# Zeros written into alpha's layout, an early ScalarE table load, and wider filler matmuls in a fused linear-attention, DFT-mixing and feed-forward kernel

## The chip, the core and the metric

The kernel runs on one core of a Trainium2 chip. Its engines are TensorE (PE in the profile; PEld is its weight load), VectorE (DVE), ScalarE (ACT), GpSimd (POOL) and SyncE (SP, which here only issues DMAs). Each takes its instructions in order from its own queue and waits on semaphores for the others. The metric is the device time of one execution in microseconds, lower being better.

## The reference, cut to what matters

```python
# attention: q, k, v, alpha are (4, 8, 768, 48); alpha lies in 0.8 .. 1.0
for t in range(768):
    state = alpha[:, :, t, :, None] * state + einsum('bhd,bhe->bhde', k[:, :, t], v[:, :, t])
    y[:, :, t] = einsum('bhd,bhde->bhe', q[:, :, t], state)
# x = y as (4, 768, 384)
mixed = real(fft(fft(x, axis=1), axis=2))
u = x + mixed
un = (u - mean(u)) / sqrt(var(u) + 1e-06)          # over the last axis
out = u + maximum(un @ w_ch1, 0.0) @ w_ch2         # 384 -> 1536 -> 384
```

## The kernel before, in words

**Tiling.** Two heads of one batch make a pair: head one on partitions 0 to 47, head two on 64 to 111 (`CW = 112` in all), time along the free axis (768 steps). There are 16 pairs, four to a batch. The recurrence is worked in chunks of `C = 64` steps. `products` (L666) builds the running product of alpha within each chunk by a scan on DVE (`w<-al,d` in the profile), then a second scan runs backwards through the alpha tile and overwrites it in place (`al<-al,back`). For both, alpha at the first step of each chunk has to be zero, so that a chunk starts afresh, and its true values have to stand in `d1`. The kernel before makes this on the chip: it copies the 12 first-step values (stride 64) into `d1`, on ACT (on DVE for pair 0), and then sets them to zero in the tile with a memset, on POOL (on DVE for pair 0). Pair 0 is loaded and worked in two halves of 384 steps.

**The check.** The scans divide by products, so the kernel first looks whether alpha is in a safe range: an ACT Square with an accumulator reads the top byte of each alpha (`c<-al,cm` in the profile, with a short instruction that reads the accumulator) and sums (top byte - 63) squared into a column of `bad`. If the sum of all is not zero, a slow general path runs after the fast one. For pairs 1 to 15 the check stands ahead of `products`; for pair 0, `check_first` (L572) loads alpha a second time into an `h` tile and checks that.

**Stages.** `attn_stages` gives a pair's stages: the scans, the products with k and q on DVE, PE transposes of k evacuated by ACT (`kt<-a`), the matmuls inside a chunk (`f<-w,al`, masked by POOL's affine_select on the copied `x`), chunk states (`f<-vn,kt`, then `tt` on DVE) and the output `y`. `mix_stages` stores the time-reversed half of y to DRAM (`scr<-y`) and gathers it back with three indirect DMAs on POOL (`y<-scr,rows`), and does both DFTs. `norm_stages` normalizes, and `ffn_stages` runs the two feed-forward matmuls (`f<-x,wt`, then `f<-wt,h`) with weights that `wsplit` prepares on ACT, DVE and POOL.

**What sets the order.** Nothing is issued as written. `Plan` (L174) records every operation with a key and an estimated duration, and `emit` (L358) lays them out on a clock of its own, engine by engine, taking what can start first and among those the lowest key. DMA bytes are costed by `wire` (L347), 400 KB per us for rows of 512 bytes and more. So a changed estimate can change the order on any engine. All instructions are issued from one helper line, L471.

**Fillers.** In the first `WARM = 120` planned us, where the plan has a gap on PE, `emit` (L430 to L432) puts `int(gap / DUMMY)` filler matmuls of zeros ahead of the next PE operation, counted at `DUMMY = 0.11` us each (the lambda at L1130, so they have their own line in the profile). A filler is an fp32 matmul and shows as two records. They write to a part of a PSUM tile that holds no result.

**The start.** On the SP queue stand, in this order: the two halves of alpha and k of pair 0, its q, its v (`vn`), then alpha, k and q, v of pairs 1, 2, 3. The ACT queue issues two small DMAs of constants. DVE begins with `setup` (L604): memsets, the first of which is `zero`, the fillers' operand.

Of the kernel before, what the change touches and what calls it, by code (L numbers as in the profile page):

```python
# [10 lines left out]
F32 = mybir.dt.float32  # L11
# [3 lines left out]
U8 = mybir.dt.uint8  # L15
I8 = mybir.dt.int8
AF = mybir.ActivationFunctionType
# [3 lines left out]
B, H, S, D = 4, 8, 768, 48  # L21
DM = H * D
DFF = 4 * DM
P = 128
NT = S // P
NP2 = H // 2
C = 64
# [3 lines left out]
CW = 112  # L31
GRP = 64
VW = NT * H // NP2 * D + GRP - D
EVAC = 5000.0
NY = 5
NAL = 4
NQK = 2
NVN = 2
# [10 lines left out]
KM = 410.0  # L49
FB = 1  # L50
PARTS = (6, 6)
SPLIT = 388
KCK = -700.0
KF0 = -505.0
WARM = 120.0
MARGIN = 0.8
DUMMY = 0.11
KTINY = 0.5 * 2.0**15 / (1.0 + 15.5 / 128.0)


# [113 lines left out]
class Plan:  # L174
# [20 lines left out]
    def fixed(self, tile):  # L195
        return View(Slot(None, tile))
# [150 lines left out]
    def wire(self, named):  # L347
        side = named["out"] if isinstance(named["out"], View) else named.get("1", named.get("in_"))
        p0, p1, _, _, n, _ = self.region(side)
        ap = side.real(self.base(side))  # L350
        size = mybir.dt.size(ap.dtype)
        return (p1 - p0) * n * size / (180e3 if ap.ap[-1][1] * size < 512 else 400e3)

    def base(self, view):
        slot = view.tile
# [2 lines left out]
    def emit(self):  # L358
# [35 lines left out]
        while placed < len(ops):  # L394
# [35 lines left out]
            if op.engine == "PE" and self.idle and t < self.idle[2] and not self.open:  # L430
                for _ in range(int((t - max(clock["PE"], self.idle[1])) / DUMMY)):
                    order.append(self.idle[0])  # L432
# [53 lines left out]


@with_exitstack
def gla_mix_ffn(ctx: ExitStack, tc: tile.TileContext, alpha, kq, v, w1, w2, consts, rowtab, out):
    nc = tc.nc  # L490
    plan = Plan({"PE": nc.tensor, "ACT": nc.scalar, "DVE": nc.vector, "POOL": nc.gpsimd, "SP": nc.sync})
    V, A, G, T, SY = (Engine(plan, e) for e in ("DVE", "ACT", "POOL", "PE", "SP"))
# [8 lines left out]
    tags = {  # L501
        "w3": ([P, 776], F32, NW3), "kt": ([P, NT - 1, CW], F32, 1),
        "z": ([P, 6, DM], F32, 1), "f": ([P, 6, DM], F32, 1), "sd": ([P, 2, 3, 2 * D], F32, 1), "h": ([P, 776], F32R, 3), "x": ([P, 776], F32R, 6),
        "y": ([P, 3, DM], F32, NY), "b8": ([P, S], I8, 1), "c8": ([P, S], I8, 1), "st": ([P, 3, 6], F32, 2), "mv": ([P, 3, 2], F32, 2),
        "r3": ([P, 3], F32, 6),
        "al": ([P, 776], F32, NAL), "kq": ([P, 2, S], F32, NQK), "vn": ([P, VW], F32, NVN), "a": ([P, 512], F32, 3), "f1": ([P, 512], F32, 2), "f2": ([P, 512], F32, 3),
    }
    count = [0]

# [15 lines left out]
    def psa():  # L525
        if state["start"]:
            state["i"] += 1
            return plan.tile(start_tags[state["i"] % 8])
        return plan.tile("a")
# [15 lines left out]
    loaded = {}  # L545
# [3 lines left out]
    d1 = fixed([P, S], "d1")  # L549
    back = fixed([P, S], "back")  # L550
    rec = fixed([P, NC], "rec")
    bad = fixed([P, B * NP2], "bad")
    cm63 = fixed([P, 1], "cm63")
    ceps = fixed([P, 1], "ceps")
    zero = fixed([P, 32], "zero")
# [3 lines left out]
    bs = fixed([P, 1], "bs")  # L559
# [3 lines left out]
    def load_first():  # L563
        t, kt, vn = plan.tile("al"), plan.tile("kq"), plan.tile("vn")
        loaded.update({("al", 0): t, ("kq", 0): kt, ("vn", 0): vn})
        for lo, o in ((0, 0), (DM, SPLIT)):
            SY.dma_start(t[:, o : o + DM], alpha[0, :, lo : lo + DM])
            SY.dma_start(kt[:, 0, lo : lo + DM], kq[0, :, 0, lo : lo + DM])
        SY.dma_start(kt[:, 1], kq[0, :, 1])
        SY.dma_start(vn, v[0])  # L570

    def check_first():  # L572
        t = plan.tile("h").bitcast(F32)
        SY.dma_start(t[:, 0:S], alpha[0])
        check(0, t)

    def check(p, t):
        top = t[0:CW, 0:S].bitcast(U8)[:, 3::4]
        A.activation(plan.tile("c8")[0:CW].bitcast(U8), top, AF.Square, bias=cm63[0:CW], accum_out=bad[0:CW, p : p + 1])

    def load_alpha(p):
        if p < B * NP2:
            t = plan.tile("al")
            loaded["al", p] = t
            SY.dma_start(t[:, 0:S], alpha[p])

    def plain(t):
        return t.rearrange("p c two n -> p (c two n)").bitcast(F32)
# [15 lines left out]
    def setup():  # L604
        V.memset(zero, 0.0)
        for hd in range(2):
            V.memset(hm[GRP * hd : GRP * (hd + 1), hd : hd + 1], 1.0)
            V.memset(hm[GRP * (1 - hd) : GRP * (2 - hd), hd : hd + 1], 0.0)
        V.memset(d1, 0.0)
        V.memset(back, 0.0)  # L610
        V.memset(back[:, C - 1 :: 2 * C], 1.0)
        V.memset(cm63, -63.0)
        V.memset(ceps, 1e-6)
        for x in mts:
            V.memset(x, 0.0)
        V.memset(ones, 1.0)
        V.memset(bad, 0.0)

    def load_consts(part):
        if part == 0:  # L620
            A.dma_start(rows, rowtab)
            A.dma_start(cst[:, ID_O:], consts[:, ID_O:])
        else:
            SY.dma_start(cst[:, :ID_O], consts[:, :ID_O])
# [35 lines left out]
    def attn_stages(b, hp, i, mixed):  # L660
        tt, mt = tts[i], mts[hp % 3]
        pair = b * NP2 + hp
# [3 lines left out]
        def products(lo, hi):  # L666
            as_, Af, o = loaded["al", pair], e["A"], off(lo)
            d, d2, chunks = d1[0:CW, lo:hi], back[0:CW, lo:hi], slice(lo // C, hi // C)
            if pair:
                A.copy(d[:, 0::C], as_[0:CW, o : o + hi - lo : C])  # L670
            else:
                same(d[:, 0::C], as_[0:CW, o : o + hi - lo : C])
            (G if pair else V).memset(as_[0:CW, o : o + hi - lo + 1 : C], 0.0)
            part = Af[0:CW, lo:hi]
            V.tensor_tensor_scan(out=part, data0=as_[0:CW, o : o + hi - lo], data1=d, initial=0.0, op0=ALU.mult, op1=ALU.add)
            r = rec[0:CW, chunks][:, 0::2]
            V.reciprocal(d2[:, 2 * C - 1 :: 2 * C], part[:, 2 * C - 1 :: 2 * C])
# [12 lines left out]

# [8 lines left out]
        def s1():  # L699
            e["A"] = w3()[:, 0:S]  # L700
            if pair:
                check(pair, loaded["al", pair])
                products(0, S)
            else:
                products(0, DM)
                times(0, R(slice(0, CW), 0, DM), 0, DM)
                products(DM, S)
# [350 lines left out]
    setup()  # L1058
    load_first()
    for p in (1, 2, 3):  # L1060
        load_alpha(p)
        load_rest(p)
    us, ress = [], [{}, {}]
    order, mixing = front(0, us, ress)
# [8 lines left out]
                    wsplit(j)  # L1073
            plan.key = key

    plan.key = KCK
    check_first()
    plan.key = -600.0
    load_weights(0)
    load_consts(1)  # L1080
# [10 lines left out]
    for i, f in enumerate(mixing()):  # L1091
        write([f], KF0 + 0.01 * i)
        n = MIX[i] if i < len(MIX) else 0
# [28 lines left out]
            write(mixing(), b * 1000 + KM)  # L1122
    plan.key = B * 1000.0
    V.tensor_reduce(out=bs, in_=bad, op=ALU.add, axis=AX.X)
    pf = psa()
    T.matmul(pf[0:1, 0:1], bs, ones, start=True, stop=True)
    V.tensor_scalar_min(fl, pf[0:1, 0:1], 1.0)
    warm = plan.tags["f2"]["reals"]
    if WARM:
        plan.idle = (lambda: nc.tensor.matmul(warm[2][0:32, 480:512], zero.real(), zero.real(), start=True, stop=True), 1.0, WARM, ("f2", 2))  # L1130
    with tc.manual_schedule():
        plan.emit()

# [102 lines left out]
def layout(q, k, v, alpha, moe_w_ch1, moe_w_ch2):  # L1236


    def pairs(x, fill):
        t = np.full((B * NP2, P, S), fill, np.float32)  # L1240
        h = x.reshape(B * NP2, 2, S, D).transpose(0, 1, 3, 2)
        t[:, 0:D], t[:, GRP:CW] = h[:, 0], h[:, 1]
        return t

    values = np.zeros((B * NP2, P, VW), np.float32)
    values[..., 0 : NT * 2 * D] = v.reshape(B * NP2, 2, NT, P, D).transpose(0, 3, 2, 1, 4).reshape(B * NP2, P, NT * 2 * D)
    return {
        "alpha": pairs(alpha, 1.0), "kq": np.stack([pairs(k, 0.0), pairs(q, 0.0)], axis=2), "v": values,
        "w1": np.ascontiguousarray(moe_w_ch1).view(np.int64), "w2": np.ascontiguousarray(moe_w_ch2).view(np.int64),
        "consts": dft_constants(), "rowtab": row_table() - DM,  # L1250
    }
# [27 lines left out]
```

## Time and profile before

| | |
|---|---|
| median of 3 runs | 534.69 us (530.01 to 540.05) |
| the profiled execution | 536.18 us, of which the span below is 534.5 us |
| mean granted TensorE clock | 0.975 |
| busy share of the span | PE 96%, DVE 65%, ACT 37%, POOL 14% |
| filler matmuls | 918 records, 38.7 us of PE |
| DMA | 44.65 MB, mean 84 GB/s |

The span runs from the first to the last instruction; the profiled execution is 1.7 us longer than its span. Fillers count as busy PE. The profile also gives the span in 40 slices of 13.4 us, with a digit for the busy share of each engine in tenths and one for the clock that was granted to TensorE. "Idle before, releaser" behind an instruction says how long its engine had stood still and whose end let it go.

### The profile page before, as it was taken

What the parts mean: (1) busy time and instruction counts of PE and PEld (TensorE: products, weight loads), DVE (VectorE), ACT (ScalarE), POOL (GpSimd) and SP (SyncE); (2) the same over time, 40 slices, a digit from 0 to 9 for tenths busy, and PEclk for the clock granted to TensorE, in tenths of its full rate; (3) what the DMA queues carried; (4) which work ended last, traced back from release to release, by engine and by line L of the source; (5) the groups of instructions that cost most, each with busy time, mean ns of one, the idle gap of its engine ahead of it and who ended that gap; (6) DMA issues with size and microseconds to landing.
All of it is one profiled execution on the core that took longest, in us unless ns stands there. A gap on an engine that the chain in (4) does not pass through costs nothing.

```text
span 534.5 us, 10290 instructions
## 1 busy us (share of the span) xinstructions
PE 511.1 (96%) x4192; PEld 491.6 (92%) x4192; DVE 347.5 (65%) x835; ACT 195.7 (37%) x425; POOL 72.7 (14%) x99
## 2 busy tenths in 40 slices
PE   6899976999999999999999999999999999999994
PEld 5898975899999999899999999999999999999994
DVE  6767998688978999877579951676367613123112
ACT  1585566443456522643332232423321413111110
POOL 0115172021311300210220000111120000000000
PEclk9699989699999999999999999999999999999999
DMA  8991216020236410142342100120021001001001
GB/s 288 411 393 34 76 45 209 0 90 24 61 102 270 156 60 1 51 143 84 134 155 75 45 0 1 45 83 25 0 90 45 2 0 45 0 1 44 1 1 50
DMA packets 17127, 44.65 MB, mean 84 GB/s; under 512 B 1905, under 2 KB 7153, under 8 KB 17073
## 3 DMA queue, kind: packets, MB, share of 16 engines
q1 hardware_dynamic: 16016, 41.49, 21.7%
q0 software_dynamic: 768, 2.36, 1.5%
q8 instruction: 35, 0.57, 0.4%
q14 instruction: 20, 0.16, 0.1%
q10 hardware_dynamic: 288, 0.07, 0.1%
HBM read 36.83 MB, written 7.08 MB: 82 GB/s over the span
## 4 chain that ended last, share of the span: by engine, by line
PE 84%; POOL 4%; issue 3%; DMA 3%; ACT 3%; DVE 2%; SPq 0%; ACTq 0%; POOLq 0%
PE f L471 59%; PE a L471 22%; POOL y L471 2%; PE f L1130 2%; DMA al<-in_alpha_dram 2%; POOL x L471 1%; DMA wt<-in_w_dram 1%; ACT b L471 1%; DVE al L471 1%; ACT x L471 1%; POOL wt L471 1%; DVE y L471 1%; SPq L471 0%; ACT wt L471 0%; DVE z L471 0%
## 5 line engine op out<-in xcount | busy, mean ns | idle before, releaser
L471 PE MATMUL f<-x,wt 128*128 128x384 f32 x864 | 181.1, 346 | 0.1
L471 PE MATMUL f<-wt,h 128*128 128x384 f32 x864 | 180.1, 343 | 0.3 <-ACT h L210 0.3
L471 PEld LDWEIGHTS f<-x,wt 128*128 128x128 f32 x864 | 151.3, 190 | 1.7 <-ACT x L471 0.5
L471 PEld LDWEIGHTS f<-wt,h 128*128 128x128 f32 x864 | 150.4, 188 | 2.1 <-ACT h L210 0.4
L471 DVE SCALAR_TENSOR_TENSOR h<-f,h 128x384 fp32r<-128x384 f32 x96 | 53.3, 556 | 112.0 <-ACT h L210 111.3
L210 ACT ACTIVATE h<-f 128x384 fp32r<-128x384 f32 x96 | 47.0, 491 | 182.1 <-PE f L471 177.3
L471 POOL TENSOR_SCALAR_AFFINE_SELECT w<-w 128x384 f32<-128x384 f32 x48 | 27.7, 598 | 159.2 <-ACT w L471 159.2
L471 PE MATMUL a<-vn,w 128*128 128x64 f32 x288 | 41.3, 265 | 0.0
L1130 PEld LDWEIGHTS f<-zero 128*32 128x32 f32 x918 | 35.5, 122 | 5.7 <-issue 1.4
L1130 PE MATMUL f<-zero 128*32 128x32 f32 x918 | 38.7, 206 | 1.6 <-DVE zero L471 1.0
L471 PEld LDWEIGHTS a<-vn,w 128*128 128x128 f32 x288 | 39.6, 191 | 0.0
L471 ACT COPY w<-a 128x384 f32<-128x384 f32 (+4 forms) x60 | 26.7, 481 | 33.8 <-PE a L471 33.7
L471 DVE TENSOR_TENSOR sd<-y,y 128x288 f32<-128x288 f32 x32 | 13.6, 464 | 29.0 <-ACT y L471 28.9
L471 DVE TENSOR_TENSOR_SCAN w<-al,d 112x768 f32<-112x768 f32 (+1 forms) x17 | 28.5, 1675 | 4.0 <-POOL al L471 4.0
L471 POOL DMA_INDIRECT y<-scr,rows x12 | 23.2, 1936 | 44.0 <-DMA scr<-y 22.0
L471 DVE TENSOR_TENSOR_SCAN al<-al,back 112x768 f32<-112x768 f32 (+1 forms) x17 | 28.2, 1660 | 0.0
L471 PE MATMUL a<-tt,w 112*128 112x96 f32 x144 | 27.6, 279 | 0.3 <-DVE tt L471 0.3
L471 DVE TENSOR_TENSOR y<-y,a 128x191 f32<-128x191 f32 (+2 forms) x88 | 25.8, 344 | 0.9 <-PE a L471 0.7
L471 PE MATMUL a<-w,al 48*128 48x128 f32 (+1 forms) x306 | 25.9, 291 | 0.0
L471 PEld LDWEIGHTS a<-w,al 48*128 48x128 f32 (+1 forms) x306 | 20.0, 187 | 5.4 <-issue 2.0
L471 DVE TENSOR_TENSOR y<-y,f 128x384 f32<-128x384 f32 (+2 forms) x46 | 20.7, 481 | 5.7 <-PE f L471 5.7
L471 PEld LDWEIGHTS a<-tt,w 112*128 112x128 f32 x144 | 23.0, 190 | 1.1 <-DVE tt L471 0.4
(118 smaller groups left out, 576.9 us busy)
## 6 DMA issues: line engine op xcount, KB each, us to landing
kq<-in_kq_dram SPq DMA_DIRECT2D x13, 768.0 KB, 4.9
wt<-in_w_dram SPq DMA_DIRECT2D x8, 768.0 KB, 8.1
al<-in_alpha_dram SPq DMA_DIRECT2D x15, 384.0 KB, 5.0
out_dram<-y SPq DMA_DIRECT2D x24, 192.0 KB, 1.9
vn<-in_v_dram SPq DMA_DIRECT2D x14, 296.0 KB, 3.3
wt<-in_w_dram SPq DMA_DIRECT2D x8, 384.0 KB, 7.4
scr<-y SPq DMA_DIRECT2D x4, 576.0 KB, 3.7
wt<-in_kq_dram SPq DMA_DIRECT2D x2, 768.0 KB, 11.2
```

The lines of the kernel that those rows point to most:

```text
L210: return lambda out, x: e.activation(out, x, AF.Relu)
L471: op.ins = op.fns[op.engine](*[real(a) for a in op.args], **{k: real(x) for k, x in op.kwargs.items()})
L1130: plan.idle = (lambda: nc.tensor.matmul(warm[2][0:32, 480:512], zero.real(), zero.real(), start=True, stop=True), 1.0, WARM, ("f2", 2))
```

## The change

Alpha gets a second copy in DRAM, `chunked`, laid out on the host. In it the first step of each chunk is zero, a zero follows the last step, and the true first-step values stand behind that, 6 for a half of pair 0 and 12 for another pair; a row is `AW = 784` elements. The kernel loads this copy. `products` copies the first-step values from there, and its memset is gone. The check now stands behind that copy, over all 128 partitions and over the zeros too, which `BADZ` takes off the sum at the end; pair 0 is checked half by half, and its second load of alpha is gone. `load_alpha(1)` moves ahead of the load of `vn` for pair 0. `setup` ends with a Square of one column of `zero` on ACT, so that ACT's table is loaded there. A filler now has 128 moving columns in place of 32 and is counted at 0.25 us; its output is columns 384 to 511 of the same PSUM tile. `wire` counts rows of 512 to 2047 bytes at 290 KB per us.

```diff
-SPLIT = 388
-KCK = -700.0
+SPLIT = 392
+AW = 784
+BADZ = 209 * 63.0**2
-DUMMY = 0.11
+DUMMY = 0.25
...
-        return (p1 - p0) * n * size / (180e3 if ap.ap[-1][1] * size < 512 else 400e3)
+        row = ap.ap[-1][1] * size
+        return (p1 - p0) * n * size / (180e3 if row < 512 else 290e3 if row < 2048 else 400e3)
...
     def load_first():
-        for lo, o in ((0, 0), (DM, SPLIT)):
-            SY.dma_start(t[:, o : o + DM], alpha[0, :, lo : lo + DM])
+        for i, lo in enumerate((0, DM)):
+            o = i * SPLIT
+            SY.dma_start(t[:, o : o + SPLIT], chunked[0, :, o : o + SPLIT])
             SY.dma_start(kt[:, 0, lo : lo + DM], kq[0, :, 0, lo : lo + DM])
         SY.dma_start(kt[:, 1], kq[0, :, 1])
+        load_alpha(1)
         SY.dma_start(vn, v[0])
-    def check_first():
-        t = plan.tile("h").bitcast(F32)
-        SY.dma_start(t[:, 0:S], alpha[0])
-        check(0, t)
-
-    def check(p, t):
-        top = t[0:CW, 0:S].bitcast(U8)[:, 3::4]
-        A.activation(plan.tile("c8")[0:CW].bitcast(U8), top, AF.Square, bias=cm63[0:CW], accum_out=bad[0:CW, p : p + 1])
+    def check(col, t):
+        n = t_width(t)
+        A.activation(
+            plan.tile("c8")[:, 0:n].bitcast(U8), t.bitcast(U8)[:, 3::4], AF.Square, bias=cm63, accum_out=bad[:, col : col + 1]
+        )
...
-            SY.dma_start(t[:, 0:S], alpha[p])
+            SY.dma_start(t, chunked[p])
...
         V.memset(bad, 0.0)
+        A.activation(zero[:, 0:1], zero[:, 0:1], AF.Square)
...
+            end = o + hi - lo + 1 + (hi - lo) // C
             if pair:
-                A.copy(d[:, 0::C], as_[0:CW, o : o + hi - lo : C])
+                A.copy(d[:, 0::C], as_[0:CW, o + hi - lo + 1 : end])
             else:
-                same(d[:, 0::C], as_[0:CW, o : o + hi - lo : C])
-            (G if pair else V).memset(as_[0:CW, o : o + hi - lo + 1 : C], 0.0)
+                same(d[:, 0::C], as_[0:CW, o + hi - lo + 1 : end])
+            check(pair + 1 if pair or lo else 0, as_[:, o:end])
...
             if pair:
-                check(pair, loaded["al", pair])
                 products(0, S)
...
     for p in (1, 2, 3):
-        load_alpha(p)
+        if p > 1:
+            load_alpha(p)
         load_rest(p)
...
-    plan.key = KCK
-    check_first()
...
     V.tensor_reduce(out=bs, in_=bad, op=ALU.add, axis=AX.X)
+    V.tensor_scalar_add(bs, bs, -BADZ)
...
-        plan.idle = (lambda: nc.tensor.matmul(warm[2][0:32, 480:512], zero.real(), zero.real(), start=True, stop=True), 1.0, WARM, ("f2", 2))
+        plan.idle = (lambda: nc.tensor.matmul(warm[2][0:32, 384:512], zero.real(), zero.real()[:, 0:1].broadcast_to([P, P]), start=True, stop=True), 1.0, WARM, ("f2", 2))
```

On the host, `layout` adds for each pair the same rows with zeros and appended values:

```python
part = raw[p, :, i * n : (i + 1) * n]
chunked[p, :, o : o + n] = part
chunked[p, :, o : o + n : C] = 0.0
chunked[p, :, o + n + 1 : o + n + 1 + n // C] = part[:, 0::C]
```

More of the change, by code (lines that the diff above doesn't have):

```diff
@@ L488, in gla_mix_ffn @@
 @with_exitstack
-def gla_mix_ffn(ctx: ExitStack, tc: tile.TileContext, alpha, kq, v, w1, w2, consts, rowtab, out):
+def gla_mix_ffn(ctx: ExitStack, tc: tile.TileContext, alpha, chunked, kq, v, w1, w2, consts, rowtab, out):
     nc = tc.nc
@@ L503, in gla_mix_ffn @@
         "z": ([P, 6, DM], F32, 1), "f": ([P, 6, DM], F32, 1), "sd": ([P, 2, 3, 2 * D], F32, 1), "h": ([P, 776], F32R, 3), "x": ([P, 776], F32R, 6),
-        "y": ([P, 3, DM], F32, NY), "b8": ([P, S], I8, 1), "c8": ([P, S], I8, 1), "st": ([P, 3, 6], F32, 2), "mv": ([P, 3, 2], F32, 2),
+        "y": ([P, 3, DM], F32, NY), "b8": ([P, S], I8, 1), "c8": ([P, AW], I8, 1), "st": ([P, 3, 6], F32, 2), "mv": ([P, 3, 2], F32, 2),
         "r3": ([P, 3], F32, 6),
-        "al": ([P, 776], F32, NAL), "kq": ([P, 2, S], F32, NQK), "vn": ([P, VW], F32, NVN), "a": ([P, 512], F32, 3), "f1": ([P, 512], F32, 2), "f2": ([P, 512], F32, 3),
+        "al": ([P, AW], F32, NAL), "kq": ([P, 2, S], F32, NQK), "vn": ([P, VW], F32, NVN), "a": ([P, 512], F32, 3), "f1": ([P, 512], F32, 2), "f2": ([P, 512], F32, 3),
     }
@@ L551, in gla_mix_ffn @@
     rec = fixed([P, NC], "rec")
-    bad = fixed([P, B * NP2], "bad")
+    bad = fixed([P, B * NP2 + 1], "bad")
     cm63 = fixed([P, 1], "cm63")
@@ L565, in load_first, with t_width @@
         loaded.update({("al", 0): t, ("kq", 0): kt, ("vn", 0): vn})
-        for lo, o in ((0, 0), (DM, SPLIT)):
-            SY.dma_start(t[:, o : o + DM], alpha[0, :, lo : lo + DM])
+        for i, lo in enumerate((0, DM)):
+            o = i * SPLIT
+            SY.dma_start(t[:, o : o + SPLIT], chunked[0, :, o : o + SPLIT])
             SY.dma_start(kt[:, 0, lo : lo + DM], kq[0, :, 0, lo : lo + DM])
         SY.dma_start(kt[:, 1], kq[0, :, 1])
+        load_alpha(1)
         SY.dma_start(vn, v[0])
-    def check_first():
-        t = plan.tile("h").bitcast(F32)
-        SY.dma_start(t[:, 0:S], alpha[0])
-        check(0, t)
-    def check(p, t):
-        top = t[0:CW, 0:S].bitcast(U8)[:, 3::4]
-        A.activation(plan.tile("c8")[0:CW].bitcast(U8), top, AF.Square, bias=cm63[0:CW], accum_out=bad[0:CW, p : p + 1])
+    def check(col, t):
[3 more added lines that the diff above has]
+        )
+    def t_width(t):
+        return plan.region(t)[4]
     def load_alpha(p):
@@ L1246, in layout @@
     values[..., 0 : NT * 2 * D] = v.reshape(B * NP2, 2, NT, P, D).transpose(0, 3, 2, 1, 4).reshape(B * NP2, P, NT * 2 * D)
+    raw = pairs(alpha, 1.0)
+    chunked = np.zeros((B * NP2, P, AW), np.float32)
+    for p in range(B * NP2):
+        for i, o in enumerate((0, SPLIT) if p == 0 else (0,)):
+            n = DM if p == 0 else S
+            part = raw[p, :, i * n : (i + 1) * n]
+            chunked[p, :, o : o + n] = part
+            chunked[p, :, o : o + n : C] = 0.0
+            chunked[p, :, o + n + 1 : o + n + 1 + n // C] = part[:, 0::C]
     return {
-        "alpha": pairs(alpha, 1.0), "kq": np.stack([pairs(k, 0.0), pairs(q, 0.0)], axis=2), "v": values,
+        "alpha": raw, "chunked": chunked, "kq": np.stack([pairs(k, 0.0), pairs(q, 0.0)], axis=2), "v": values,
         "w1": np.ascontiguousarray(moe_w_ch1).view(np.int64), "w2": np.ascontiguousarray(moe_w_ch2).view(np.int64),
```

## The prediction, made before the changed kernel was built or run

> **What bounds the kernel now.** I read the page's 40 slices and its chain by engine first.
>
> ```profile
> PE   6899976999999999999999999999999999999994
> DVE  6767998688978999877579951676367613123112
> PEclk9699989699999999999999999999999999999999
> ...
> PE 84%; POOL 4%; issue 3%; DMA 3%; ACT 3%; DVE 2%; SPq 0%; ACTq 0%; POOLq 0%
> ```
>
> From slice 8 on (about 107 us) TensorE is full and has its full clock: there the time is its own work, which the change does not touch. What can move is the first 100 us, where DVE is fullest and PE has gaps, and where the clock falls in slices 1, 5 and 7 (counted from 0, 13.4 us each). So I read the chain of waits and the list by time there.
>
> ```profile
> 3.64 8.27 DMA al<-in_alpha_dram
> 11.98 1.28 ACT L471
> 13.28 1.03 ACT c L471 x2
> ...
> 6.99 0.51 PE L471 MATMUL a<-cst,al 112*128 112x112 f32 x3
> 7.43 1.64 PE L1130 MATMUL f<-zero 128*32 128x32 f32 x46
> ...
> 14.21 0.20 ACT L471 COPY d<-al 112x12 f32<-112x12 f32 x1
> 14.31 0.43 ACT L471 COPY kt<-a 128x336 f32<-128x336 f32 x1
> 14.46 0.12 POOL L471 MEMSET al<- 112x13 f32 x1 [13.93 <-ACT d L471]
> 14.62 1.76 DVE L471 TENSOR_TENSOR_SCAN w<-al,d 112x768 f32<-112x768 f32 x1 [3.97 <-POOL al L471]
> ...
> 14.79 1.43 PE L471 MATMUL f<-vn,kt 128*112 128x96 f32 x6 [5.72 <-ACT kt L471]
> ```
>
> Pair 1's alpha lands at 3.64 + 8.27 = 11.91. Only then does ACT load its table (1.28), run the check (1.03), copy the first steps, and POOL zero them; DVE stands still 3.97 us until 14.62 and PE 5.72 until 14.79, as pair 0's kt copy is queued behind the check. This stall is the change's target.
>
> **The change part by part.** The profiled execution took 536.18, 1.5 above the median 534.69; the sum is made against it and then lowered by 1.5.
>
> *A, the start.* From landing to scan is 14.62 - 11.91 = 2.71 us. Of that only the copy and the crossing to the next engine stay: 0.35 (estimate: POOL begins 0.25 behind the copy's start, and I add 0.1). That saves 2.35. The load also comes earlier, since the v of pair 0 now stands behind it:
>
> ```profile
> vn<-in_v_dram SPq DMA_DIRECT2D x14, 296.0 KB, 3.3
> ...
> h<-in_alpha_dram SPq DMA_DIRECT2D x1, 384.0 KB, 8.9
> ...
> 10.00:20.00 10.00, 5.21 (x36) 4.65 (x37) 4.84 (x8) 5.53 (x13) 1.11 (x3) 0.66 1.02 412
> ```
>
> 296 KB at 412 GB/s (the last column; DMA share 1.02, so full) is 0.74 us. Both make 3.1; bounds are 2.35 (landing unmoved) and 3.97 (the whole idle). PE gains less: the check may still stand ahead of the kt copy, so kt moves from 14.31 to about 11.2 + 0.2 + 1.03 = 12.4, by 1.9. PE's side is in B; here I take DVE's **3.1**. v itself lands later by 384 KB, 0.95 us; pair 0's state matmul waits for kt longer than that. Dropping the second alpha load gives all later loads 0.95 us, and takes a whole check (1.03) off ACT; I saw no wait for weights in the list before 61 us, so both are costed at nothing; if the bus set the pace there, up to 0.95 more. Pair 0's two half checks cost ACT at most twice that check, while it otherwise waits for pair 1. Should they be late, DVE's backward scan of pair 0 is queued behind them. The other 14 memsets (0.12 us each, on a POOL that waited 13.93 for this one) and rows wider by 2% move nothing. DVE loses two memsets of 7 columns and gains one tiny add at the end, nothing either way.
>
> *B, fillers at the start.* Two rows size one filler now and then.
>
> ```profile
> L1130 PE MATMUL f<-zero 128*32 128x32 f32 x918 | 38.7, 206 | 1.6 <-DVE zero L471 1.0 <-ACT x L471 0.6
> ...
> L471 PE MATMUL a<-cst,z 128*96 128x128 f32 x56 | 7.5, 276 | 0.0
> ...
> 1.04 6.02 PE L1130 MATMUL f<-zero 128*32 128x32 f32 x116 [1.04 <-DVE zero L471]
> ...
> 1.26 0.46 ACTq L471 DMA_DIRECT2D cst<-in_consts_dram  x1
> ```
>
> Today's filler takes 38.7 / 459 = 0.084 us over all, counted 0.11. A record with 128 moving columns takes 7.5 / 56 = 0.134 (the row is of that shape alone), so a new filler is about 0.26 warm and 0.52 at half clock, counted 0.25: warm it fills a planned gap, cold it runs to twice its length. The first 58 fillers stand for 6.4 planned us, so some 25 new ones. They now wait for `zero` from ACT: after its DMA issue at 1.72, 1.28 of table and 0.2 of Square, so 3.2 in place of 1.04. Today's 58 at 0.104 beside the 23 at 1.64 / 23 = 0.071 say that the array is slow for the first 4 to 5 us. So 9 fillers run cold (4.7) and 16 warm (4.2), and PE's first real work goes from 6.99 to about 12.1, its 0.51 to 12.6: just where A has the kt copy. Behind it stand the next 10 (46 records, 2.5 planned, 2.6 real), so the state matmuls start near 15.2, 0.4 later than today. But no idle is left, and the idle of 5.72 costs the clock today:
>
> ```profile
> 12.00:14.00 2.00, 0.00 (x0) 0.00 (x0) 0.00 (x0) 1.99 (x2) 0.00 (x0) 0.81 1.03 426
> 14.00:16.00 2.00, 1.21 (x6) 1.21 (x7) 1.39 (x1) 1.13 (x6) 0.12 (x1) 0.50 1.02 413
> ...
> 22.00:24.00 2.00, 2.00 (x36) 1.89 (x35) 2.00 (x4) 1.03 (x3) 0.00 (x0) 0.63 1.05 407
> ...
> 16.77 2.93 PE L471 MATMUL f<-w,al 64*128 64x128 f32 x24
> ...
> 20.81 0.66 DVE L471 TENSOR_TENSOR tt<-f,mh 112x480 f32<-112x480 f32 x1 [1.96 <-ACT d L471]
> ...
> 27.36 1.61 PE L471 MATMUL f<-w,al 64*128 64x128 f32 x24
> ```
>
> The clock is half from about 13.2 to 23; the same 24 matmuls take 2.93 cold and 1.61 warm. The state that DVE waits for needs those in the list from 14.79 to 20.7, 5.9 us; warm about 3.1. So PE hands it over at 18.3 in place of 20.7, where DVE by A alone could take it at 17.7 (20.81 - 3.1). That is 0.6 late, up to 3.4 if the clock stays half (15.2 + 5.9), and -1.96 is the other end, were today's wait to vanish: **+0.5**.
>
> The Trainium skill, "ScalarE: Activation LUTs", section "What ACT_TABLE_LOAD costs", gives a switch as about 1283 ns of load plus 1380 ns of drain. The trace agrees with the first (1.28) and shows no second: the check starts at 13.28, right as the load ends. By that page `zero` and all fillers would come 1.4 us later still, PE's state matmuls with them, and B would be 1.9 in place of 0.5: 533.0, inside the forecast's own case. I go by the row.
>
> *C, the gap ahead of the feed-forward.*
>
> ```profile
> 70.63 5.54 PE L471 MATMUL f<-cst,z 128*97 128x65 f32 x36 [2.90 <-DVE z L471]
> ...
> 81.35 5.63 PE L1130 MATMUL f<-zero 128*32 128x32 f32 x172
> 91.73 0.90 PE L471 MATMUL f<-cst,f 128*128 128x128 f32 x3 [4.75 <-ACT f L471]
> 95.59 1.28 PE L1130 MATMUL f<-zero 128*32 128x32 f32 x20 [0.58 <-ACT x L471]
> 97.73 1.17 PE L1130 MATMUL f<-zero 128*32 128x32 f32 x18
> 98.83 4.47 PE L471 MATMUL f<-x,wt 128*128 128x384 f32 x16
> ...
> 92.00:94.00 2.00, 2.00 (x14) 1.27 (x13) 2.00 (x5) 2.00 (x5) 0.00 (x0) 0.50 0.04 8
> ...
> L471 PE MATMUL f<-x,wt 128*128 128x384 f32 x864 | 181.1, 346 | 0.1
> ```
>
> 86 fillers (9.5 planned us) end at 86.98; after 4.75 idle PE starts the feed-forward at half clock. New: 37 fillers of 0.26 end near 91.0, leaving 0.7 idle. If the clock holds, 16 matmuls of 4.47 become 16 x 181.1 / 864 = 3.35, saving 1.1, and the 19 fillers at 95.59 and 97.73 (2.45 us) become 7 of 0.26 (1.8), saving 0.65; the transposes before them gain up to half of 0.90 each, part of it behind ACT. If it falls, 7 cold ones take 3.6, a loss of 1.2. Between 3.0 and -1.2 I take **2.0**. The gap before 70.63 fills likewise, but there PE waits for DVE, as the row says: nothing.
>
> The Trainium skill, "TensorE: Matmul & The Clock Gate", section "Why this matters for your kernels", asks for no idle over about 3 us. Our 2.90 idle before 70.63 did cost the clock (slice 5 of the page's clock row has an 8), so the trace is a little stricter; by either 0.7 is safe and C stands.
>
> *D, fillers between pairs.*
>
> ```profile
> 20.00:60.00 40.00, 12.58 (x274) 10.91 (x275) 0.96 0.54 211
> ...
> 36.99 2.72 PE L1130 MATMUL f<-zero 128*32 128x32 f32 x80
> 39.96 0.46 PE L471 MATMUL a<-tt,w 112*128 112x96 f32 x2 [0.26 <-DVE tt L471]
> ```
>
> The first row is of the fillers alone: 137, standing for 15.1 planned us, took 12.58. New ones are at most 60, 15.6 us warm. Where work stood right behind, they overrun: the 40 at 36.99 become 17, 4.4 us, 1.4 past the 2.98 until DVE let PE go. If all of it were on the path, 3.0; if none, 0, or a little less than nothing where short gaps now get no filler: **+1.5**.
>
> *E, the plan's order.* The new DMA and filler estimates can reorder every engine. No row shows that; I put 0, with 4 us either way, the size of the largest single stalls above.
>
> Sum: 536.2 - 3.1 + 0.5 - 2.0 + 1.5 = 533.1; less 1.5, **531.6 us**.
>
> **The rivals.**
>
> *The gain is swallowed behind 61 us.* The feed-forward's start is a chain through POOL:
>
> ```profile
> 64.77 6.72 POOL L471 DMA_INDIRECT y<-scr,rows  x1 [12.59 <-DMA scr<-y]
> 71.79 1.62 POOL L471 DMA_INDIRECT y<-scr,rows  x1 [0.31 <-issue]
> ```
>
> Two gathers of the same size take 6.72 and 1.62, so their time depends on what runs beside them. Should they grow by what A and B leave, 2.6 us: 534.2. For: it is on the chain. Against: all of it hangs on y, which comes earlier.
>
> *Slower: fillers on a cold clock.* If PE falls to half clock between 20 and 60 us, 60 fillers of 0.52 take 31 us against 12.58, 18.6 more, and PE's real work queues behind them. A, B and C together give 4.6, so it decides once a quarter of that lies on the path; with half there, 9.3: 536.2 - 4.6 + 9.3 - 1.5 = 539.4. For: cold fillers run to twice their count. Against: that stretch has clock 0.96 today, cold only until 23.
>
> *The wider filler does not hold the clock.* Were the gap before 91.73 longer, or its fillers fewer, C would be a loss of 1.2 in place of 2.0: 534.8. For: an idle of 2.90 lost it. Against: 0.7 of idle is planned.
>
> *Faster by more.* The whole 3.97 and 1.96 go, C gives 3.0, D nothing: 536.2 - 8.9 - 1.5 = 525.8; with 2 to 3 us of better order 523.
>
> **How the numbers follow.** Forecast 0.45 (528 to 534.5); swallowed 0.20; clock not held 0.08; slower 0.15; faster 0.12. The range, 525 to 539, leaves out about a half of the faster and of the slower case and the tails of the order. A measurement of this kernel tells about 2% from no change, that is under 524.0 or over 545.4: faster 0.09 (part of that case and a lucky order), slower 0.03, same 0.88.
>
> **What would show it.** A right: the scan of pair 1 starts near 11.5, with under 1.5 us of DVE idle before it, and no table load behind the alpha DMA. B right: fillers begin near 3.2, the state matmuls near 15, and the clock is 1.00 from 13 to 23. C right: idle of about 1 us ahead of the feed-forward's transposes, clock 1.00 at their start, the 16 matmuls in 3.4. D: fillers between 20 and 60 us near 15 us in all. All together: PE full from about 96 in place of 98.8. Wrong would be: a feed-forward start that did not move though the scan did (swallowed), half clock between 24 and 60 (slower), or an order of stages on DVE or POOL that no longer resembles today's.

## The result, and the profile after

The changed kernel takes 537.33 us (median of 20 runs, 536.17 to 539.17 and one of 636.68), the kernel before 534.83 beside it (20 runs, 530.01 to 542.31). The ratio is 1.0086, 95% interval 1.0068 to 1.0104: slower by about 0.9%, where a gain of 0.6% was forecast (531.6). The time lies inside the range of 525 to 539 and inside the 2%, but on the other side. The unchanged kernel has runs near 542 beside its usual 530 to 535; here and below the comparison leaves such disturbed runs of both kernels out, so a ratio is not that of the two medians beside it.

The profiled execution of the changed kernel took 537.70 (span 535.9). From its page the rows of PE, DVE and the granted clock in 40 slices, and the chain by engine and by line:

```profile
PE   7999999899999999999999999999999999999995
DVE  8867898879988999766569962677466713113212
PEclk9999999799999999999999999999999999999998
...
PE 90%; DVE 5%; ACT 2%; DMA 1%; issue 0%; ACTq 0%; SPq 0%
```

PE is now at 90% or more from slice 1 on (counted from 0), but for slice 7 and the last, and so is the clock. Before, POOL, DMA and ACT held 10% of the chain; now PE holds 90% of it. So the clock is held as intended, and the time still rose: a part of what fills PE is not the kernel's work. The list of groups on the same page says of what; 410 records are 205 fillers:

```profile
L1135 PE MATMUL f<-zero 128*32 128x128 f32 x410 | 54.4, 286 | 6.0 <-ACT zero L473 3.3
```

54.4 us in place of 38.7. One filler takes 54.4 / 205 = 0.265 over all. That this is the prediction's 0.26 is chance, as that was meant for a warm one: the 25 at the start take 7.62 / 25 = 0.305, the 37 ahead of the feed-forward 8.41 / 37 = 0.227. The list by time of the first 65 us (start, duration, engine, line, operation; in brackets the idle time before and what ended it):

```profile
1.75 1.28 ACT L473 ACT_TABLE_LOAD   x1 [1.75 <-PEq L1283]
3.05 0.20 ACT L473 ACTIVATE zero<-zero 128x1 f32<-128x1 f32 x1
3.30 7.62 PE L1135 MATMUL f<-zero 128*32 128x128 f32 x50 [3.30 <-ACT zero L473]
...
10.40 1.75 DVE L473 TENSOR_TENSOR_SCAN w<-al,d 112x768 f32<-112x768 f32 x1
10.85 0.51 PE L473 MATMUL a<-cst,al 112*128 112x112 f32 x3
11.29 2.19 PE L1135 MATMUL f<-zero 128*32 128x128 f32 x18
...
14.36 1.61 PE L473 MATMUL f<-w,al 64*128 64x128 f32 x24
15.89 0.63 PE L473 MATMUL f<-vn,kt 128*112 128x96 f32 x4
...
17.09 1.87 DVE L473 TENSOR_TENSOR_SCAN w<-al,d 112x768 f32<-112x768 f32 x1 [2.47 <-ACT d L473]
18.87 0.62 DVE L473 TENSOR_TENSOR tt<-f,mh 112x480 f32<-112x480 f32 x1
19.52 1.52 PE L1135 MATMUL f<-zero 128*32 128x128 f32 x12
...
22.26 1.96 PE L1135 MATMUL f<-zero 128*32 128x128 f32 x16
24.15 0.46 PE L473 MATMUL a<-tt,w 112*128 112x96 f32 x2
...
27.36 0.40 ACT L473 COPY y<-a 128x288 f32<-128x288 f32 x1 [2.25 <-PE a L473]
...
64.71 0.40 ACT L473 COPY y<-f 128x288 f32<-128x288 f32 x1 [0.93 <-PE f L473]
```

The start came much as forecast: the table is loaded while nothing waits for it, the scan of pair 1 starts at 10.40 with no idle of DVE ahead of it, the 24 matmuls run warm (1.61), and DVE takes the state at 18.87 (forecast 18.3). Two things differ. PE has the state ready at 15.89 + 0.63 = 16.52, but DVE first stands still for 2.47 us and then runs pair 2's scan: the stall moved on from pair 1 to pair 2, whose copy of the first-step values ends only at 17.05 on ACT. And PE's fillers stand behind the state: the product that reads it (`a<-tt,w`) starts at 24.15, 4.7 us after DVE's step ended (18.87 + 0.62). In the run without fillers (e3, below) the same product starts at 18.11, right behind that step (17.39 + 0.62). The first y copy comes at 27.36 in place of 27.01, and the last one at 64.71 in place of 60.75.

How much of this is the change, and how much the one execution shown of before? The kernel before was profiled once more in the study (run g4, 531.03). From its list by time:

```profile
9.49 1.28 ACT L471 ACT_TABLE_LOAD   x1 [9.49 <-DMA al<-in_alpha_dram]
...
12.12 1.76 DVE L471 TENSOR_TENSOR_SCAN w<-al,d 112x768 f32<-112x768 f32 x1 [1.53 <-POOL al L471]
...
23.68 0.40 ACT L471 COPY y<-a 128x288 f32<-128x288 f32 x1 [1.02 <-PE a L471]
...
57.44 0.40 ACT L471 COPY y<-f 128x288 f32<-128x288 f32 x1
...
88.37 0.85 PE L471 MATMUL f<-cst,f 128*128 128x128 f32 x3 [4.69 <-ACT f L471]
...
95.39 3.06 PE L471 MATMUL f<-x,wt 128*128 128x384 f32 x16
```

In this execution pair 1's alpha landed 2.4 us earlier (9.49 against 11.9), the stall of DVE that the change aims at is 1.53 and not 3.97, and the clock is back before the 16 matmuls (3.06 and not 4.47). The three stretches of half clock are all still there; the first and the third are shorter (13.4 to 20.2 and 88.5 to 95.3 us). The marks of the three executions:

| mark, us | before, as shown | before, again | after |
|---|---|---|---|
| scan of pair 1 starts | 14.62 | 12.12 | 10.40 |
| DVE takes pair 0's state | 20.81 | 17.47 | 18.87 |
| first y copy | 27.01 | 23.68 | 27.36 |
| last y copy | 60.75 | 57.44 | 64.71 |
| first transposes of the feed-forward | 91.73 | 88.37 | 92.91 |
| first matmul of its second layer | 104.54 | 99.68 | 107.54 |
| span | 534.5 | 529.3 | 535.9 |

From first to last y copy both executions of before take 33.7 to 33.8, the changed kernel 37.35; from the transposes to the second layer they take 12.81 and 11.31, the changed kernel 14.63. These two stretches, and against the second execution the part up to the first y copy (27.36 against 23.68), are where the time went. The list of PE around the transposes:

```profile
83.70 8.41 PE L1135 MATMUL f<-zero 128*32 128x128 f32 x74
92.91 1.74 PE L473 MATMUL f<-cst,f 128*128 128x128 f32 x9 [0.80 <-ACT f L473]
96.54 1.91 PE L1135 MATMUL f<-zero 128*32 128x128 f32 x8 [1.89 <-ACT x L473]
98.39 1.01 PE L473 MATMUL f<-x,wt 128*128 128x384 f32 x2
99.33 1.49 PE L1135 MATMUL f<-zero 128*32 128x128 f32 x6
100.75 4.00 PE L473 MATMUL f<-x,wt 128*128 128x384 f32 x16
```

And its windows there (the clock is the third number from the end):

```profile
92.00:94.00 2.00, 1.14 (x7) 0.62 (x6) 2.00 (x10) 1.85 (x4) 0.00 (x0) 1.00 0.01 3
94.00:96.00 2.00, 0.60 (x4) 0.31 (x3) 2.00 (x7) 2.00 (x5) 0.00 (x0) 1.00 0.00 0
96.00:98.00 2.00, 1.46 (x7) 1.24 (x8) 1.32 (x4) 2.00 (x7) 0.00 (x0) 0.50 0.00 0
```

The fillers end at 92.11 with the planned idle of 0.80 behind them. But then PE does nothing but nine records of transposes until 96.54, and at 96.0 the clock falls to half. The 4 + 3 fillers behind (8 and 6 records) cost 3.40 at half clock, ahead of the feed-forward, and the 16 matmuls take 4.00.

### The profile page after: what moved, and what is told of

It is laid out like the page before. It is cut to its first block, busy times and chain, and to the rows that moved or that the text cites. A ratio compares the mean times of both kernels' runs of the same rounds, so it can differ in the third digit from the quotient of the medians.

```text
span 535.9 us, 9241 instructions
## 1 busy us (share of the span) xinstructions
PE 522.1 (97%) x3684; PEld 496.5 (93%) x3684; DVE 350.4 (65%) x834; ACT 196.7 (37%) x428; POOL 70.1 (13%) x84
## 4 chain that ended last, share of the span: by engine, by line
PE 90%; DVE 5%; ACT 2%; DMA 1%; issue 0%; ACTq 0%; SPq 0%
PE f L473 60%; PE a L473 24%; PE f L1135 6%; DVE wt L473 1%; DVE z L473 1%; DVE w L473 1%; DMA wt<-in_w_dram 1%; ACT x L473 1%; DVE y L473 0%; ACT L473 0%; DVE f L473 0%; DVE sd L473 0%; ACT b L473 0%; ACT f L473 0%; ACT c L473 0%
## 5 line engine op out<-in xcount | busy, mean ns | idle before, releaser
L1135 PE MATMUL f<-zero 128*32 128x128 f32 x410 | 54.4, 286 | 6.0 <-ACT zero L473 3.3
L473 POOL TENSOR_SCALAR_AFFINE_SELECT w<-w 128x384 f32<-128x384 f32 x48 | 28.9, 622 | 236.1 <-ACT w L473 236.1
L1135 PEld LDWEIGHTS f<-zero 128*32 128x32 f32 x410 | 44.6, 114 | 10.7 <-ACT x L473 3.4
L473 DVE TENSOR_TENSOR_SCAN w<-al,d 112x768 f32<-112x768 f32 (+1 forms) x17 | 29.9, 1758 | 2.5 <-ACT d L473 2.5
```

What stands on the lines that cost most here:

```text
L473: op.ins = op.fns[op.engine](*[real(a) for a in op.args], **{k: real(x) for k, x in op.kwargs.items()})
L1135: plan.idle = (lambda: nc.tensor.matmul(warm[2][0:32, 384:512], zero.real(), zero.real()[:, 0:1].broadcast_to([P, P]), start=True, stop=Tr ...
```

## The experiments

Three causes stood against each other: the wide fillers themselves (Theory 1), the new order of the plan (Theory 2), and, from the second group on, the lateness of the first fillers, which gaps filled to the brim never give back (Theory 3). Where an expectation gives a number to a theory, it is one of these. Fillers do not count on the plan's own clock, so an edit of the fillers alone leaves the order of all other work as it is.

**First group: fillers against the rest.** Old fillers in the changed kernel:

```diff
-DUMMY = 0.25
+DUMMY = 0.11
-... warm[2][0:32, 384:512], zero.real(), zero.real()[:, 0:1].broadcast_to([P, P]) ...
+... warm[2][0:32, 480:512], zero.real(), zero.real() ...
```

> The changed kernel with the fillers of before (32 moving columns, counted 0.11 us); fillers take no time on the plan's clock, so the order of all other work is that of the changed kernel. Theory 1 (the wide fillers stand in front of PE's real work between 17 and 65 us and eat what the early scan won): pair 1's scan stays near 10.4 us, pair 0's first y copy on ACT comes at 23 to 25 in place of 27.4, the 16 feed-forward matmuls start at 95 to 98 in place of 100.8, time 0.985 to 0.998 of before. Theory 2 (the new layout and DMA estimates gave a worse order, the fillers are about neutral): first y copy still at 27, feed-forward still near 100, time 1.005 to 1.012 of before.

Measured: 537.51 (6 runs), ratio 1.0006 [0.9969, 1.0043], between the ranges of the two theories. With its old fillers the rest of the change shows no gain. The new fillers in the kernel before (the same edit the other way):

> The kernel before with the wide fillers alone (128 moving columns, counted 0.25 us); all other work in the order of before. Theory 1 (wide fillers delay real work): PE is full of fillers and work without idle from 17 to 65 us, the last y copy of batch 0 comes 2 to 4 us after 60.8, time 1.003 to 1.010 of before. Theory 2 (the order is the cause, fillers neutral or good for the clock): the gap before 91.7 keeps the clock full, feed-forward 1 to 2 us earlier, time 0.995 to 1.000 of before.

Measured: 534.04, 1.0031 [0.9999, 1.0062]. The fillers alone do not make the 0.9% either. By the marks, its first y copy comes at 23.47 and its last at 58.53: with the new fillers in the old order these lie 35.06 apart, 1.3 more than before. No fillers at all in the changed kernel (`WARM = 0.0`):

> The changed kernel without any filler. Theory 1: between 17 and 65 us nothing stands in front of real work, but PE is at half clock for most of the first 100 us; first y copy on ACT at 24 to 27, feed-forward started cold, time 0.995 to 1.010 of before, and slower than the changed kernel with the fillers of before. Theory 2: fillers matter little to the order; time 1.008 to 1.02 of before, the loss of the clock on top of the worse order.

Measured: 533.69, 1.0023 [0.9992, 1.0054], faster than with them, at a mean clock of 0.941 in place of 0.991: holding the clock cost more than the clock gave. Half as many (`DUMMY = 0.50`):

> The changed kernel with the wide filler counted at 0.50 us, so half as many stand in each gap. Theory 1: about half of the filler time on the path goes, time 0.993 to 1.003 of before, and idle after the fillers ahead of the feed-forward of about 5 us, so that the clock falls there. Theory 2: time as the changed kernel, 1.005 to 1.012 of before.

Measured: 537.52, 1.012 [1.0068, 1.0172], at the upper edge of Theory 2 and against Theory 1. Half of them no longer hold the clock: its mean is 0.963, and 0.75 between the first and the last y copy, which lie 40.28 apart.

**Second group: where fillers hurt.** The first fillers from 4.5 us on in place of 1.0, so that some 11 in place of 25 stand ahead of the first transposes:

```diff
-..., start=True, stop=True), 1.0, WARM, ("f2", 2))
+..., start=True, stop=True), 4.5, WARM, ("f2", 2))
```

> The changed kernel with the first gap's fillers counted from 4.5 planned us in place of 1.0: 11 fillers in place of 25 ahead of PE's first work, all else and its order the same. Theory 3 (the early fillers end late, since they wait for ACT's table load and run on a cold array, and as a wide filler now fills each planned gap to the brim no later gap gives that lateness back): PE's first transposes start near 8 in place of 10.9, pair 0's y copy on ACT at 24 to 25 in place of 27.4, batch 0's last at 61.5 to 63 in place of 64.7, the 16 feed-forward matmuls at 97.5 to 99.5 in place of 100.8, time 0.998 to 1.004 of before. Theory 2 (the order of the new plan is the cause): first transposes early, but the last y copy within 1 us of 64.7 and time 1.006 to 1.011.

Measured: 535.0 (12 runs), 1.0042 [1.0015, 1.0069]: half of the loss is gone. Its list by time:

```profile
7.51 0.51 PE L473 MATMUL a<-cst,al 112*128 112x112 f32 x3
...
25.05 0.40 ACT L473 COPY y<-a 128x288 f32<-128x288 f32 x1
...
62.40 0.40 ACT L473 COPY y<-f 128x288 f32<-128x288 f32 x1 [0.92 <-PE f L473]
```

PE's first work comes 3.34 earlier, and the first and the last y copy each exactly 2.31 earlier: the 37 us between them, with all their gaps, gave nothing of the start's lateness back. That is Theory 3; the time (1.0042) lies just above the 1.004 that was given for it. The same from the other side, no table load at the start (the one line `A.activation(zero...)` taken out, so the fillers need not wait for ACT):

> The changed kernel without the early table load, in the same order: fillers need not wait for ACT, the table load comes ahead of pair 0's first check. Theory 3: fillers start at 1.0 in place of 3.3, PE's first transposes at 8.7 in place of 10.9, the last y copy of batch 0 some 2 us earlier than 64.7, time 1.000 to 1.006 of before. Theory 2: no change of the late part, 1.006 to 1.011; or slower still, if the table load delays the check that DVE's backward scan of pair 0 waits for.

Measured: 534.94, 1.0046 [1.0029, 1.0063]; its y copies come at 24.98 and 62.33, both 2.38 earlier than after's. A reserve of 0.8 us in each planned gap:

```diff
-for _ in range(int((t - max(clock["PE"], self.idle[1])) / DUMMY)):
+for _ in range(int((t - max(clock["PE"], self.idle[1]) - 0.8) / DUMMY)):
```

> The changed kernel with 0.8 us of each planned gap left empty: 135 fillers in place of 205, none in the short gaps, the order of all else the same. Theory 3: the first work still starts near 10, but the lateness is given back in the next gaps; first y copy at 24 to 26, last at 60 to 62, the 16 feed-forward matmuls at 96 to 98.5, time 0.993 to 1.001 of before, if the clock holds between 17 and 65 us. Theory 2: 1.004 to 1.010.

Measured: 532.29, 0.9992 [0.9965, 1.002]: the whole loss is gone, although its clock is half from 43 to 60 and from 91 to 101. The y copies come at 25.12 and 62.51, so with this clock the stretch between them is not shorter (37.39); the last one was expected at 60 to 62. The old DMA estimate (400e3 for all rows of 512 B or more), which leads to another order:

> The changed kernel with the DMA estimate of before (400 KB per us for all rows of 512 bytes and more): a somewhat different plan, with 203 fillers. Theory 3: the same lateness, time 1.005 to 1.012 of before. Theory 2 in its narrow form (the DMA estimate made the worse order): 0.995 to 1.003.

Measured: 536.41, 1.0063 [1.0036, 1.0091], its interval overlaps that of the change, and the 0.995 to 1.003 of the narrow Theory 2 is ruled out: the estimate is at most a small part of the cause.

**Third group: the feed-forward, and a better version.** f1, and no fillers planned behind 88 us, which takes away the 16 that stand from the feed-forward's transposes on (`WARM = 88.0`):

> The changed kernel with fillers counted from 4.5 planned us, and none after 88 planned us, that is, none from the feed-forward's first transposes on (16 fewer); the order of all else unchanged. Theory 3, second part (behind the transposes the clock falls in any case, so that the fillers there run at half clock, up to 0.48 us each, in front of the first feed-forward matmuls): the y copies stay where they are with fillers from 4.5 (25.0 to 62.4), the first 18 feed-forward matmuls start near 95 in place of 95.4 and 97.7 and are done by 101 to 102, and the second half's first matmuls come near 102 in place of 104.1; time 0.998 to 1.001 of before. Rival: those fillers only stood in gaps that DVE and ACT leave; time as with fillers from 4.5, 1.002 to 1.006.

Measured: 531.44, 0.9988 [0.9968, 1.0007] against f1's 1.0042: these fillers cost half a per cent. With a reserve of 0.4 us beside it:

> As the run before it, and 0.4 us of each planned gap left empty. Theory 3: what lateness arises is given back in the next gap, and the clock still holds between 17 and 65 us more than with 0.8 left empty; last y copy at 60 to 61.5, time 0.993 to 0.999 of before, the fastest of this study. Rival: as the run before it, within 0.002; or slower, if the clock falls between 40 and 58 us as it did with 0.8 left empty.

Measured: 529.01, 0.9937 [0.9903, 0.9971], faster than both kernels. The filler time between 20 and 50 us (windows of the filler's line alone; duration, busy PE with its records) in f1 and in g2, which have the same order of all other work:

```profile
20.00:50.00 30.00, 10.84 (x78) 7.53 (x78) 1.00 0.68 264
```

```profile
20.00:50.00 30.00, 4.89 (x34) 3.24 (x34) 1.00 0.66 258
```

And g2's list by time:

```profile
24.35 0.39 ACT L473 COPY y<-a 128x288 f32<-128x288 f32 x1
...
56.41 0.38 ACT L473 COPY y<-f 128x288 f32<-128x288 f32 x1
...
89.85 5.29 PE L473 MATMUL f<-x,wt 128*128 128x384 f32 x18 [1.08 <-ACT x L473]
```

From first to last y copy it takes 32.06 in place of f1's 37.35. In the fixed window of 20 to 50 us there are 5.95 us less of fillers; between each run's own two copies the fillers take 11.89 in f1 and 6.47 in g2, 5.4 less for 5.3 us of time, with the clock at 1.00 in both: what stood in the gaps stood on the path. The kernel before without fillers (`WARM = 0.0`), and the kernel before as it is, for one more profile:

> The kernel before without any filler, in its own order: beside the changed kernel without fillers (1.0023 of before, interval 0.9992 to 1.0054) it shows what layout, check, load order and estimates do by themselves. If the early scan's gain reaches the feed-forward when no filler stands in the way: 1.006 to 1.012, the feed-forward starting some 3 us later than the 95.2 of the changed kernel without fillers. If the gain is lost in the order of the stages behind it, fillers or not: 0.998 to 1.004 and a start within 1 us of 95.2.

> The kernel before, profiled once more, to see how far its own profile moves: if it is a quicker execution than the one shown (536.18 us), the clock should be full in one or two of the three stretches where it was half (13 to 23, 71 to 75, 92 to 102 us), and the 16 feed-forward matmuls should start near 96 in place of 98.8; the part from there to the end should stay at about 435 us.

Measured: 527.81 (6 runs), 0.9904 [0.988, 0.9929], and 531.03 for the single run of the second. The first was not expected: the fillers cost the kernel before 1% as well, although without them its mean clock is 0.95. And it turned the question round: without fillers the changed kernel takes 1.0023, the kernel before 0.9904, so something beside the fillers costs 1.2%. By the marks of e3 against g3, the scan of pair 1 is earlier (10.50 against 12.39), but the first y copy is later (23.82 against 21.60), the way from it to the last one longer (37.38 against 34.37), and so is the way from the transposes to the second layer (10.26 against 8.58); only from the last y copy to the transposes is it shorter (30.76 against 32.45).

**Fourth group: what beside the fillers.** In the changed kernel the plan puts pair 2's scans on DVE ahead of pair 0's state steps. One dependence more, without fillers, puts them behind the first state step, as in the kernel before:

```diff
+scans = [n for n, op in enumerate(ops) if op.name == "tensor_tensor_scan"]
+steps = [n for n, op in enumerate(ops) if op.name == "scalar_tensor_tensor" and isinstance(op.kwargs.get("scalar"), View)]
+ops[steps[0]].users.append(scans[6])
+ops[scans[6]].left += 1
```

> The changed kernel without fillers, and one dependence more in the plan: pair 2's forward scan behind the first state step of pair 0, where the kernel before has it. Theory of the order (without the copy, check and memset ahead of it the plan finds pair 2's scan ready and puts it and the backward scan ahead of pair 0's state steps; DVE hands the state over late, PE stands idle 1.8 us at 18.9 and falls to half clock): the first state step comes near 18 in place of 20.34, the first y copy near 21 in place of 23.82, the full clock lasts past 24, and the time falls from 533.7 to 528 to 530 (ratio 0.990 to 0.995). Rival (the 1.2% between the two orders without fillers lie elsewhere: in the order behind 30 us, or in the loads): the first y copy comes earlier all the same, but the time stays at 532 to 535.

Measured: 533.81 (12 runs), 1.0032 [0.9996, 1.0069]: no gain, against the theory of the order and as its rival had it. The list by time, of e3 first, then of h1:

```profile
23.82 0.38 ACT L473 COPY y<-a 128x288 f32<-128x288 f32 x1
...
61.20 0.38 ACT L473 COPY y<-f 128x288 f32<-128x288 f32 x1
```

```profile
18.26 0.41 ACT L477 COPY y<-a 128x288 f32<-128x288 f32 x1
...
67.47 0.40 ACT L477 COPY y<-f 128x288 f32<-128x288 f32 x1 [0.15 <-PE f L477]
```

The first y copy came 5.6 earlier, more than expected, and the last one 6.3 later. In h1 the clock is half from 24.6 to 82.6; the execution shown took 538.07, 4.3 above the median of its runs. The fillers of g2 in the kernel before, so that both orders stand under the same fillers:

> The kernel before with the fillers of the run g2: 128 moving columns counted 0.25, from 4.5 us on, none planned behind 88 us, 0.4 us of each planned gap left open. So the two orders stand under the same kind of fillers, both warm. If the rest of the change is worth something by itself once the clock is full (its scan starts 4 us earlier), this comes out above g2: 531 to 533. If the new order costs with a full clock too: 525 to 528. If it costs only through the clock: 528 to 530, as g2.

Measured: 531.9, 0.9967 [0.9934, 0.9999] against g2's 0.9937 [0.9903, 0.9971]. The intervals overlap; with these fillers neither order is shown to be better. g2 with the dependence of h1:

> The run g2 with the same dependence as h1. Theory of the order: the first y copy near 21 to 22 in place of 24.35, and 526 to 528 in place of 529.0. If a full clock hides the order, 528.5 to 530.

Measured: 529.5, 0.9946 [0.9916, 0.9977], as g2. And two parts of the change alone, without fillers in the kernel before:

```diff
     V.memset(bad, 0.0)
+    A.activation(zero[:, 0:1], zero[:, 0:1], AF.Square)
...
     SY.dma_start(kt[:, 1], kq[0, :, 1])
+    load_alpha(1)
     SY.dma_start(vn, v[0])
```

> The kernel before without fillers, with two parts of the change alone: the table loaded at the start, and pair 1's alpha ahead of pair 0's v. The scan of pair 1 then starts near 11 in place of 12.39. If that gain reaches the end: 526 to 527 in place of 527.8; if it is swallowed by the order that the plan makes of it, 527.5 to 530.

Measured: 531.3, 0.9978 [0.9937, 1.0019], not faster than g3 (0.9904 [0.988, 0.9929]) and by the intervals a little slower: the gain does not reach the end. Its scan of pair 1 starts at 10.87 (g3: 12.39), DVE takes the state at 16.80 (17.86), and yet the first y copy comes at 22.04 (21.60): the early gain is lost within 12 us, ahead of any clock change that the record shows in either (it falls near 23 and near 27).

What these runs say of the 1.2%: windows from 20 to 104 us of g3, h4, e3 and h1, in this order (the clock is the third number from the end):

```profile
20.00:104.00 84.00, 55.86 (x399) 51.30 (x397) 74.76 (x180) 52.90 (x103) 25.38 (x23) 0.72 0.42 150
```

```profile
20.00:104.00 84.00, 55.92 (x390) 51.70 (x386) 72.05 (x179) 53.13 (x103) 23.46 (x23) 0.74 0.42 152
```

```profile
20.00:104.00 84.00, 58.89 (x355) 53.50 (x356) 70.76 (x173) 49.79 (x94) 21.96 (x17) 0.64 0.40 144
```

```profile
20.00:104.00 84.00, 56.08 (x299) 50.99 (x298) 64.97 (x165) 45.18 (x83) 22.44 (x17) 0.57 0.40 145
```

Clock 0.72, 0.74, 0.64, 0.57 stand beside spans of 526.7, 527.2, 532.5 and 536.4. Without fillers the time goes with how long PE keeps its clock, and the kernel before's order keeps it longer in these; with g2's fillers no difference is shown. That fits four executions; whether the order causes the clock, or both follow from a third thing, stays open, as does which part of the change sets that order.

## Why the prediction was wrong

The sum, stage by stage (from the table of marks), against the shown execution of before and against the second one (g4):

| stage | predicted | measured | against g4 |
|---|---|---|---|
| up to the first y copy (terms A and B) | -2.6 | +0.35 | +3.7 |
| first to last y copy (D) | +1.5 | +3.6 | +3.6 |
| last y copy to the transposes (E) | 0 (4 either way) | -2.8 | -2.7 |
| transposes to the second layer (C) | -2.0 | +1.8 | +3.3 |
| behind it | 0 | -1.6 | -1.3 |
| sum | -3.1 | +1.4 | +6.6 |

The measured loss, 0.9% or about 4.6 us, lies between the two sums.

**A was right in its mechanism and too large in its base.** The scan starts where it was forecast or earlier (10.40; "near 11.5"), with no table load behind the load of alpha. But the prediction took 3.97 us of stall, in one profiled execution, for the kernel's. There alpha landed at 11.9; in the profiled executions of e2, g3 and g4 the table load that waits for it starts at 9.94, 9.75 and 9.49, and g4's stall is 1.53. The scan's gain is 4.2 against the shown execution and 1.7 against g4. "Less 1.5" at the end took the difference to the median off as if it lay elsewhere; a part of it may have been this very stall, which differs by 2.4 between the two executions. And the prediction did not follow DVE beyond pair 1: 2.47 us of idle came back ahead of pair 2's scan.

**B failed at its end.** Fillers start at 3.30 (forecast 3.2), PE's first work at 10.85 (12.1), its state matmuls at 13.40 (15.2), the clock is full from 13 to 23, and DVE takes the state at 18.87 (18.3). That last agreement is luck: PE was done with the state at 16.52, 1.8 earlier than forecast, and DVE took it late because pair 2's scan stood first. The step that failed was to stop there, as if what PE hands over at 18.3 were the end of the stage. Behind it stood 24 more fillers up to the y copy, and PE, whose first work came 3.3 later than in f1, found no open gap to make that good. f1 and f2 show it: 2.3 (f1) and 2.4 us (f2) earlier at the first y copy are as much earlier at the last.

**D was mis-sized: 1.5 predicted, 3.6 measured, outside its own bound of 3.0.** The filler time between 20 and 60 was right ("near 15 us in all"; 14.62 in the windows of the filler's line). Between the two y copies the fillers take 11.89 in place of 9.47, 2.4 more; PE's other work there takes 25.1 in place of 23.7, so 1.4 of the 3.6 is work that the new order put into this stretch, which the prediction had at nothing (E). In the old order (e2) the new fillers lengthen the stretch by 1.3, near the forecast. So two steps failed: the fillers' part was sized too small for the new order (1.5 against 2.4), and the order was taken to add nothing. Besides, the prediction took as a cost only filler time beyond before's 12.58, and not what full gaps do to lateness. The gaps of the plan are estimates, and an estimate's slack is used by whatever comes late. Before, a warm filler counted 0.11 took 0.07 in a long row (2.72 / 40), so a gap kept more than a third of its length open; now six take 1.52 and eight 1.96, counted 1.5 and 2.0, and next to nothing stays open for the lateness of the start. g2 against f1 prices it: 5.4 us less of fillers, 5.3 us less of path.

**C had the wrong sign.** The idle ahead of the transposes is 0.80, as forecast (0.7), and the clock is 1.00 at their start. The step that failed was to let the transposes keep it: between the last filler's end (92.11) and the next one (96.54) there are only nine records of transposes, and the clock falls at 96.0. It falls there in g1 too, at 93.0, 3.1 us after the last filler, with the same nine transposes in between. "If it falls, 7 cold ones take 3.6, a loss of 1.2" was then right in kind (3.40 measured). So the rival "the wider filler does not hold the clock" is the one that came true of C, but not for its reason, idle. g1 shows that these fillers are better left out. The Trainium skill, "TensorE: Matmul & The Clock Gate", section "Part 4: PE-mode transpose", says that a transpose on TensorE does not count as busy in the same way, and that the full clock does not engage for it. The windows above agree with that, and by it the 0.80 us of idle on which C rested becomes the 4.4 from 92.11 to 96.54. The prediction had weighed only that page's rule on idle. That transposes count for nothing is not shown: 1.74 us of any work may have been too little.

**E is where the bound was needed.** The -2.8 between the last y copy and the transposes goes with the rest of the change and not with the fillers: with the new fillers in both the stretch takes 28.20 in the changed kernel and 32.18 in e2, with none 30.76 in e3 and 32.45 in g3. Which part of the change does it, and where the -1.6 behind the second layer comes from, no run shows.

**The other rivals.** Swallowed behind 61 us: no. The three gathers take 5.61 + 1.63 + 5.36 = 12.6 against 6.72 + 1.62 + 4.17 = 12.5. Fillers on a cold clock: no, the clock is 1.00 from 20 to 60. The time rose instead with warm fillers, and with an order of the plan that costs 1.2% without any. Of the marks given ahead, "PE full from about 96 in place of 98.8" was the one that showed it: 100.75.

## What to carry to other kernels

A filler that takes as long as it is counted turns an estimated gap into fixed time: lateness at one place is then carried, us for us, through the stretch behind it (f1, f2), so leave a part of each gap open (g2) and let none stand just ahead of work on the path (g1). Ask what a held clock costs: in the kernel before, leaving all fillers out was faster (0.9904) in spite of the lower clock. And before a stall is counted as a term, look whether a second execution has it at the same size.

## What the runs showed of the hardware that was not expected

- Nine transposes did not hold the clock: it fell 3.9 us after the last filler, with 1.74 us of transposes and 2.15 of idle in between, and in g1 3.1 us after it, with the same transposes in between.
- The same load of alpha, behind the same loads, let the table load start at 9.49 in one execution of the unchanged kernel and at 11.98 in another, 2.5 us apart, and 3.4 of lateness were still there at the first transposes of the feed-forward (88.37 against 91.73).
- A granted clock of 1.00 at the start of a record is not always a full clock. In g3, without fillers, it reads 1.00 up to about 27 us. Its list by time has the same 24 matmuls twice in that stretch:

```profile
14.30 2.89 PE L471 MATMUL f<-w,al 64*128 64x128 f32 x24
...
20.82 1.61 PE L471 MATMUL f<-w,al 64*128 64x128 f32 x24
```

The first ones run at half speed, as the 2.93 did in the shown execution at a granted 0.50. The durations are the safer reading there.
